# Queries turned in f32, and expert 0's token weights as six rows: a change at the start of an attention and mixture-of-experts kernel

## The chip, the cores and the metric

The kernel runs on one core of one Trainium2 chip. The core has a matrix engine (TensorE, PE in the profile; its weight loads are listed apart as PEld), VectorE (DVE), ScalarE (ACT), GpSimd (POOL) and SyncE (SP). Each works through its own list of instructions in order; semaphores hold one engine until another, or a DMA, is done. DMAs are issued from SP's queue or from POOL's queue here (a single one from ACT's) and are carried by 16 DMA engines. Loads that change the number format on the way (f32 in memory, f16 in the core) are issued from POOL. The metric is device microseconds for one execution; lower is better.

## The reference

The program computes a block-sorted attention and feeds its result to a small mixture of experts:

```python
# attention: B, H, S, D = 4, 8, 768, 64; 8 blocks of 96 rows
P = sort_net                                   # (4, 8, 8, 8)
for _ in range(5):                             # Sinkhorn
    P = exp(P - max(P, -1))
    P = P / sum(P, -1)
    P = P / sum(P, -2)
k_sorted, v_sorted = P @ k_blocks, P @ v_blocks        # mixes whole blocks
attn = softmax(q_blocks @ k_sorted.T / sqrt(D))
x = (attn @ v_sorted)                          # laid out as (3072, 512)
# experts: E, D, F = 4, 512, 1024
p = domain_probs / sum(domain_probs, -1)       # (3072, 4)
out = sum over e of p[:, e] * (relu(x @ w1[e]) @ w2[e])
```

## The kernel before

The order of the instructions is written out by hand; no planner moves them. The work goes through batch elements 0 to 3 one after the other, and inside each through "pairs" or "quads" of heads. Attention of batch element 0 has its own code at the start, in half-blocks, so that the first expert matmuls can begin early; later batch elements' attention is woven between the expert matmuls of the one before. Towards the end only expert matmuls are left.

The change touches only what happens in the first 12 us, before the first attention matmul. There the program does this:

- SP issues, in this order, the load of `sn` (the sorting network, L77), of `p_in` (the domain probabilities with 24 tokens on each partition, L170) and of `p_own` (L171): the probabilities of batch element 0's 768 tokens, placed so that token number t*128+p is on partition p. In `p_own` each piece in memory is the four probabilities of one token, 16 bytes, so this load has 768 pieces.
- POOL issues `load_half_queries(0)` (L172; two loads by L152, one for heads 0 to 3 and one for heads 4 to 7, each 64 partitions with four heads' rows, cast to f16 into `q0`, which lives in the memory of the later tile `Tt[3]`), then `load_natural(0, "k", 0)`, builds the identity `ident`, and issues the loads of `v` for quad 0, `k` and `v` for quad 1, and the four pieces of expert 0's first weight matrix (L183). Then it builds masks (L191 to L200) and, from L330, one half of `sn16`. A load on POOL's queue uses one of eight semaphores in turn, so each waits for the one eight before it.
- TensorE runs `warm(84)` (L307, the matmuls are at L276): matmuls on a constant whose result nobody reads. Inside the fifth Sinkhorn round it transposes the first half of the queries (`h_q(0, 0)` and `h_q(1, 0)`, 24 transposes each at L288, f16) and runs `warm(30)`. ScalarE copies each result into `qT0` (L292).
- VectorE and ScalarE run the five Sinkhorn rounds (L310 to L321): an exponential on ScalarE, then two reductions, two reciprocals and two products on VectorE. Between the rounds VectorE does a step of `spread_weights` (L246, L248, L250: the experts' token weights for all tokens, from `p_in`).
- After the fifth round VectorE and POOL each build a half of `sn16` (L330). `r_half(0)` (L379, matmuls at L342) spreads the first half over 128 partitions into the PSUM tile `ps_R`; VectorE's `build_PI0` (L353) makes the mixing matrices from it; and `mix_half` (L521) multiplies `k` and `v` by them. From there TensorE, VectorE and ScalarE hand the work to and fro until the expert matmuls come in (L704 from 18.6 us on).
- `own_weights` (L261 to L266, called at L1435) turns `p_own` into `p_sb`, expert 0's weight for each token of batch element 0. Its product is first used when VectorE evacuates expert 0's output (L748, 31 us).
- `load_half_queries(1)` (L1405) brings the other half of the queries later.

PSUM tiles come from two rings of two buffers each, `psM` (which holds the warm-up tiles, `ps_R` and some of the mixes) and `psA` (which holds the transposed queries and others). The large tile `room` is free until 36 us, when it takes expert 0's output.

## Time and profile before

| what | value |
|---|---|
| median of three runs | 358.08 us (358.04 to 359.21) |
| the profiled execution's own time | 358.21 us |
| its span, first to last instruction | 356.3 us |
| TensorE matmul busy | 350.4 us (98%) |
| VectorE busy | 277.5 us (78%) |
| ScalarE busy | 170.1 us (48%) |
| POOL busy | 137.6 us (39%) |
| granted TensorE clock | 1.00 |
| TensorE busy in 0 to 5, 5 to 10, 10 to 12 us | 3.94, 5.00, 0.76 us |
| DMA landings: `k` quad 0, `v` quad 0, `k` quad 1, `v` quad 1 | 10.3, 12.2, 14.2, 16.1 us |

The span is what the profiler sees between the first and the last instruction; the execution's time is some 1.9 us longer. A busy share is an average over the whole run, so the table says little about the first 12 us, which is a mere 3% of it. For a stage as short as this one the instructions have to be read one after the other, with the column that says how long an engine was idle before an instruction and what ended that idle time. A matmul row's length is that of a whole group; matmuls overlap, so the spacing between them is shorter than the length of one.

### The profile page before, as it was taken

Reading aid. Unit: us, or ns where it says so; the run is one execution under the profiler, and the core shown is the slowest. Engines: PE = TensorE matmul, PEld = TensorE weight load, DVE = VectorE, ACT = ScalarE, POOL = GpSimd, SP = SyncE. Lnnn points to the kernel's source line nnn. Section 1 sums busy time; section 2 is a strip of 40 time slices with the busy share of each in tenths; the row PEclk is TensorE's granted clock in tenths of the full one; section 3 lists DMA queues with packets and bytes.
Section 4 is the critical chain, followed back from the end, with each engine's and each line's share of the span. In section 5 each row is a group of like instructions: output and inputs, shape, how many; then the busy total and the mean of one; then the engine's idle time right before and its main releaser. Section 6 shows DMA issues by size and latency. Waiting matters only on the chain.

```text
span 356.3 us, 9511 instructions
## 1 busy us (share of the span) xinstructions
PE 350.4 (98%) x3948; PEld 305.5 (86%) x3948; DVE 277.5 (78%) x555; ACT 170.1 (48%) x302; POOL 137.6 (39%) x154
## 2 busy tenths in 40 slices
PE   8899999999999999999999999999999999999996
PEld 8686857888888888988899888888888888888886
DVE  5766787779798687778879988896678886588963
ACT  2653330452425445368847259830288611598301
POOL 8766112466022420000626318840068800188400
PEclk9999999999999999999999999999999999999999
DMA  8999999999999999743995410005200014100021
GB/s 104 203 205 230 212 209 194 207 195 167 195 180 166 195 116 203 138 88 44 180 205 91 107 74 0 2 1 136 78 26 3 2 37 141 62 0 2 0 75 46
DMA packets 74762, 40.26 MB, mean 113 GB/s; under 512 B 41568, under 2 KB 70496, under 8 KB 74720
## 3 DMA queue, kind: packets, MB, share of 16 engines
q0 software_dynamic: 38720, 19.93, 43.2%
q1 hardware_dynamic: 35856, 19.67, 27.2%
q8 instruction: 31, 0.51, 0.6%
q14 instruction: 11, 0.09, 0.1%
q10 hardware_dynamic: 144, 0.07, 0.1%
HBM read 41.88 MB, written 6.34 MB: 135 GB/s over the span
## 4 chain that ended last, share of the span: by engine, by line
PE 95%; DVE 3%; issue 0%; DMA 0%; ACT 0%; DVEq 0%
PE ps_h L815 18%; PE ps_Q L1296 18%; PE ps_p L799 12%; PE ps_X L1153 10%; PE ps_Z L1153 7%; PE ps_Q L1153 7%; PE ps_Z L1296 6%; PE ps_h L704 3%; PE ps_o L741 3%; PE ps_p L860 3%; PE ps_a L479 2%; PE ps_s L444 2%; PE ps_k L425 1%; PE ps_v L391 1%; PE ps_mv L521 1%; PE ps_a L593 0%
## 5 line engine op out<-in xcount | busy, mean ns | idle before, releaser
L815 PE MATMUL ps_h<-xT,w 128*128 128x256 f16 x576 | 67.5, 273 | 0.0
L815 PEld LDWEIGHTS <-w 128*128 128x128 f16 x576 | 55.2, 98 | 7.3
L821 DVE SCALAR_TENSOR_TENSOR Hb<-ps_h,pb 128x1024 f16<-128x1024 f32 x34 | 41.5, 1223 | 17.8 <-PE ps_h L815 17.6
L1153 PEld LDWEIGHTS <-w 128*128 128x128 f16 x480 | 43.6, 98 | 4.7
L1166 POOL TENSOR_TENSOR arena<-tmp,pb 128x512 f16<-128x512 f32 x12 | 15.2, 1276 | 65.7 <-PE ps_Z L1153 49.8
L1296 PEld LDWEIGHTS <-Hb 128*128 128x128 f16 x320 | 31.1, 98 | 3.5
L1165 ACT ACTIVATE tmp<-tmp 128x512 f32<-128x512 f32 x46 | 29.0, 632 | 3.9 <-DVE tmp L1203 3.9
L1296 PEld LDWEIGHTS <-Sb 128*128 128x128 f16 x304 | 28.2, 98 | 3.0
L1153 PEld LDWEIGHTS <-arena 128*128 128x128 f16 x312 | 27.7, 98 | 2.8
L451 ACT ACTIVATE ET<-ps_s 96x768 f16<-96x768 f32 x24 | 18.1, 802 | 25.2 <-PE ps_s L444 25.0
L434 ACT CAST kT<-ps_k 64x384 f16<-64x384 f32 x48 | 22.7, 473 | 13.3 <-PE ps_k L425 12.3
L126 POOL DMA_DIRECT2D arena<-in_q_dram x24 | 19.9, 842 | 20.8 <-DMA q_ring<-arena 17.7
L1153 PE MATMUL ps_X<-ET,arena 128*128 128x256 f16 x168 | 25.2, 272 | 0.0
L1296 PE MATMUL ps_Q<-w,Hb 128*128 128x256 f16 x192 | 24.6, 273 | 0.0
L799 PEld LDWEIGHTS <-Hb 128*128 128x128 f16 x232 | 21.9, 98 | 3.0
L1159 DVE SCALAR_TENSOR_TENSOR Hb<-ps_X,pb 128x512 f16<-128x512 f32 x27 | 18.7, 692 | 7.0 <-PE ps_X L1153 7.0
L1173 ACT COPY ps_X<-ps_Z 128x512 f32<-128x512 f32 x27 | 15.4, 571 | 17.8 <-PE ps_Z L1153 17.8
L1153 PE MATMUL ps_Z<-xT,w 128*128 128x256 f16 (+1 forms) x176 | 22.5, 258 | 0.0
L785 DVE TENSOR_TENSOR Sb<-Hb 128x512 f16<-128x512 f16 x33 | 20.6, 646 | 0.0
L1180 ACT COPY tmp<-ps_X 128x512 f32<-128x512 f32 x26 | 15.2, 586 | 9.2 <-PE ps_X L1153 6.6
L1159 DVE SCALAR_TENSOR_TENSOR Hb<-ps_Z,pb 128x512 f16<-128x512 f32 x27 | 18.4, 683 | 1.3 <-PE ps_Z L1153 1.3
L1203 DVE TENSOR_TENSOR tmp<-ps_Q,tmp 128x512 f32<-128x512 f32 x26 | 17.7, 683 | 0.8 <-PE ps_Q L1153 0.8
(270 smaller groups left out, 744.3 us busy)
## 6 DMA issues: line engine op xcount, KB each, us to landing
w<-in_moe_w_dram POOLq DMA_DIRECT2D x4, 1024.0 KB, 27.2
w<-in_moe_w_dram POOLq DMA_DIRECT2D x6, 512.0 KB, 19.7
arena<-in_k_dram POOLq DMA_DIRECT2D x7, 384.0 KB, 7.6
arena<-in_v_dram POOLq DMA_DIRECT2D x7, 384.0 KB, 8.1
vs<-arena SPq DMA_DIRECT2D x36, 66.0 KB, 5.3
arena<-in_q_dram POOLq DMA_DIRECT2D x24, 96.0 KB, 7.5
out_dram<-ob SPq DMA_DIRECT2D x9, 256.0 KB, 2.0
pb<-p_dram SPq DMA_DIRECT2D x4, 512.0 KB, 5.8
```

Source lines behind the costliest of these rows:

```text
L126: nc.gpsimd.dma_start(t[:, h // 2, :, h % 2, :], q[b, h].rearrange("(t p) d -> p t d", p=P))
L434: nc.scalar.copy(kT[ds(D * hh, D), r], pk[ds(D * r, D), hh].rearrange("p a (i c) -> p a i c", c=CP),)
L451: nc.scalar.activation(ETs[2 * (pr % 2) + hh][:, 0:S].rearrange("c (a x) -> c a x", a=2), pss[hh][0:BLK, :, 0:HS], AF.Exp, bias=0.0, scale ...
L785: tt(sm[0], blk(0, 1), blk(1, 1), ALU.add)
L799: nc.tensor.matmul(ps, lhs(e, f), Ts[e][rhs][:, f, :], start=(first and e == es[0] and f == 0), stop=(done and e == es[-1] and f == KH - 1 ...
L815: nc.tensor.matmul(ps[:, f, :], w1sb[e][:, kc, ds((4 * g + f) * P, P)], xT[:, kc, ds(2 * c * P, 2 * P)], start=(kc == 0), stop=(kc == NKC ...
L821: nc.vector.scalar_tensor_tensor(out=Hb[:, homes.get(e, e), ds(4 * g, 4), :], in0=ps[:], scalar=0.0, op0=ALU.max, in1=weights(e).broadcast ...
L1153: nc.tensor.matmul(dst[:, ds(f * cols, cols)], a[lhs][:, k, ds((f0 + f) * P, P)], t[rhs][:, k, :], start=(first and f == 0 and k == 0), st ...
L1159: nc.vector.scalar_tensor_tensor(out=home(i, j), in0=src.rearrange("p (f x) -> p f x", f=m), scalar=0.0, op0=ALU.max, in1=weight(j).broadc ...
L1165: nc.scalar.activation(src, src, AF.Relu, bias=0.0, scale=1.0)
L1203: tt(t12, Q, u2, ALU.add)
L1296: nc.tensor.matmul(ps, lhs(e, f), Ts[e][rhs][:, f, part], start=(first and e == 0 and f == 0), stop=(e == E - 1 and f == KH - 1), skip_gro ...
```

## The change

Five things change, all ahead of the first attention matmul:

1. The first query half of heads 0 to 3 is no longer loaded by POOL with a cast to f16, but by SP as f32 into the same memory (`q32`), second in SP's list, ahead of the domain probabilities.
2. `p_own` is no longer loaded as 768 pieces of 16 bytes. SP loads six rows of 512 numbers (128 tokens by 4 experts each) into `room`, and four f32 matmuls (one for each expert, six rows by 128 columns against a 6x6 identity) turn them into the old layout, in an unused part of the PSUM tile `ps_R`. VectorE copies the 24 columns into `p_own`. The matmuls and the copy stand just ahead of `r_half(0)`.
3. POOL makes an f32 identity of 64x64 (`ident32`) from `ident`.
4. The 24 f16 transposes of heads 0 to 3 become 24 f32 matmuls against `ident32` (`h_q32`), which run right after the first warm-up instead of inside the fifth Sinkhorn round; ScalarE's copy converts their result to f16.
5. The warm-ups shrink from 84 to 60 and from 30 to 20 matmuls.

```diff
+    q32 = q0[0:64].rearrange("p f h r d -> p (f h r d)").bitcast(F32).rearrange("p (h r d) -> p h r d", h=4, r=R)
+    nc.sync.dma_start(q32.rearrange("p h r d -> p h (r d)"), half_queries(0, 0))
     nc.sync.dma_start(p_in, moe_domain_probs.rearrange("(p t) e -> p t e", t=NT))
-    nc.sync.dma_start(p_own, moe_domain_probs[0:S].rearrange("(t p) e -> p t e", p=P))
-    load_half_queries(0)
+    own_rows = room[0:R, 1, :].rearrange("t (p e) -> t p e", e=E)
+    nc.sync.dma_start(own_rows, moe_domain_probs[0:S].rearrange("(t p) e -> t p e", p=P))
+    nc.gpsimd.dma_start(q0[ds(64, 64), 0].rearrange("p h r d -> p h (r d)"), half_queries(1, 0))
     load_natural(0, "k", 0)
     ident = const.tile([P, P], F16, name="ident")
     make_identity(nc, ident)
+    ident32 = room[0:64, 0, 0:64]
+    nc.gpsimd.tensor_copy(ident32, ident[0:64, 0:64])
...
+    def h_q32():
+        ps = psa([P, 2, 512], F32, "ps_q32")
+        for sg in range(2):
+            for r in range(R):
+                for hh in range(2):
+                    nc.tensor.matmul(
+                        ps[ds(D * hh, D), sg, ds(r * 64, 64)], q32[:, 2 * sg + hh, r, :], ident32, start=True, stop=True
+                    )
+        return ps[:, :, 0:R * 64].rearrange("p s (r x) -> p s r x", r=R)
...
-    warm(84)
+    warm(60)
+    ps_q32 = h_q32()
...
         if it == 4:
-            for qd in range(2):
-                h_q(qd, 0, nc.scalar.copy)
-            warm(30)
+            nc.scalar.copy(qT0[0][:, :, 0], ps_q32)
+            h_q(1, 0, nc.scalar.copy)
+            warm(20)
...
+    own_ps = ps_R[:, 0, ds(256, R * E)].rearrange("p (e t) -> p e t", e=E)
+    for e in range(E):
+        nc.tensor.matmul(own_ps[:, e, :], own_rows[:, :, e], ident32[0:R, 0:R], start=True, stop=True)
+    nc.vector.tensor_copy(p_own.rearrange("p t e -> p e t"), own_ps)
     r_half(0)
```

## The prediction

> **What bounds the kernel now.** I read the page's engine shares first, then the chain that ended last, then the timeline of the first 17 us, because everything that the change touches lies there.

> ```profile
> PE 350.4 (98%) x3948; PEld 305.5 (86%) x3948; DVE 277.5 (78%) x555; ACT 170.1 (48%) x302; POOL 137.6 (39%) x154
> ...
> PE 95%; DVE 3%; issue 0%; DMA 0%; ACT 0%; DVEq 0%
> ```

> TensorE carries the end: the chain is 95% PE and no share of it is a DMA. So a saving counts only if it brings TensorE's real work forward, and a delay in front of that work counts in full. The chain's own list, in order of time (start, length, what), shows what holds the first 12 us:

> ```profile
> 0.75 1.53 DMA sn<-in_sort_net_dram
> ...
> 10.64 0.20 DVE scol L319
> 10.86 0.69 DVE sn L330
> 11.55 0.05 issue
> 11.60 0.26 PE ps_R L342 x4
> 11.86 0.55 PE ps_mk L507 x8
> ...
> 12.45 0.57 PE ps_mk L521 x24
> ```

> From the landing of `sn` to 11.55 us this is the Sinkhorn chain on VectorE and ScalarE; the change leaves all of it in place. `r_half(0)` (L342) is the first TensorE work anybody needs. What TensorE does before is warm-up and the first query transposes, with room behind them (timeline: start, length, engine, line):

> ```profile
> 5.72 0.23 DVE L246 TENSOR_REDUCE T<-T 128x24 f32<-128x96 f32 x1
> ...
> 7.73 0.85 PE L288 MATMUL ps_q<-ident,T 64*64 64x64 f16 x48
> ...
> 8.51 1.85 PE L276 MATMUL ps_w<-Hb 128*128 128x128 f16 x30
> ...
> 9.51 1.46 ACT L292 COPY Sb<-ps_q 128x768 f16<-128x768 f16 x2
> ...
> 10.86 0.68 DVE L330 TENSOR_TENSOR sn<-sn,scol 32x512 f16<-32x512 f32 x1
> ...
> 11.60 0.26 PE L342 MATMUL ps_R<-ident,sn 32*128 32x32 f16 x4 [1.24 <-DVE sn L330]
> ...
> 11.97 0.75 DVE L353 TENSOR_TENSOR Sb<-maskk,ps_R 128x256 f16<-128x256 f16 x2 [0.43 <-PE ps_R L342]
> ...
> 16.15 0.57 PE L521 MATMUL ps_mv<-Sb,arena 128*64 128x64 f16 x24
> ```

> The reader should see the 1.24 us that TensorE idles before L342, waiting for VectorE: that is the cover for everything added to TensorE here. Behind L342 there is no cover: VectorE waits for it, then TensorE for VectorE, and so on until TensorE is dense (it is busy all of the 20 us from 40 to 60).

> **The change part by part.** The sum is made against the profiled run: 358.21 us, that is a span of 356.3 and 1.9 around it; the median of the three runs is 358.08, 0.13 lower.

> *Loads.* The first q half for heads 0 to 3 leaves POOL's queue for SP's, uncast; 768 pieces of 16 bytes become six rows. POOL loses one issue (two took 1.46 us, so 0.73) and gains the copy `ident32` (nearest row: L194's copy, 128x128, 0.29), so `k0` is issued 0.73 us earlier, `v0` and all behind it 0.44. POOL's own later work (its half of L330 ended at 12.46, needed by `r_half(1)` at 13.33) moves earlier too, and nobody waits for it. In the load queue one 384 KB load follows another by 1.9 us (`k0`, `v0`, `k1`, `v1` land at 2.71+7.6=10.3, 4.13+8.1=12.2, 4.88+9.3=14.2 and 5.62+10.5=16.1), so dropping 192 KB brings each about 1.0 us forward. First uses are at 12.45, 12.82, 14.40 and 16.15, none with a wait for DMA: worth 0. If `v1`, which lands only 0.03 us before its use, or `k1` (0.2 before) did hold TensorE, the gain is 0.2 at most, because the work queued ahead of each on TensorE ends no sooner.

> On SP the new load stands ahead of the domain probabilities, whose issue slips by one issue (0.40-0.45), 1.21 to 1.66. They landed 1.8 us after issue, at 3.0; L246 can start as late as 5.87 before the Sinkhorn step behind it (6.11) slips. The 384 KB ahead of them cost between nothing and all of a load of that size: an SP store of 256 KB landed in 2.0 us, so 3.0 for this one. Landing is then between 3.5 and 1.21+3.0+1.8=6.0, a stall of 0 to 0.15. I take 0, since the queue was nearly empty then (30 GB/s between 2.5 and 3.0 us). The six rows are needed only near 10 us.

> *Queries on TensorE.* Removed: 24 of 84 and 10 of 30 warm-up matmuls and 24 f16 transposes. Added: 24 f32 matmuls, 64x64, each loading its own weights. Of the 84 warm-ups 38 start in the first 5 us, and the other 46 take 7.63-5.0=2.63, 57 ns each; 60 of them end at 5.0+22x0.057=6.25. No f32 matmul is in this trace. Lower bound: no dearer than an f16 transpose, 0.85/48=18 ns, 0.43 us for 24. Upper bound: weight load and matmul of one transpose, nothing overlapped, 0.11+0.19=0.30 us, 7.2 us. I take 0.11 each, 2.6 us: the length of one 64x64 weight load, since in the built order these matmuls have no weight load of their own that could run ahead, while nothing says that the streaming behind the load is serial too.

> [...]

> Then 24 transposes (0.43), 20 warm-ups (20x57 ns=1.14) and the four matmuls that turn expert 0's weights. Those: as little as L342's spacing, (0.26-0.17)/3=0.03 each, at most 0.12+0.17=0.29 unoverlapped; I take one 128-column weight load, 0.12, so 0.5 of between 0.1 and 1.2. TensorE is through at 6.25+2.6+0.43+1.14+0.5, with 0.15 for the last matmul's way to PSUM: 11.1, between 8.5 and 16.4. It must be through by 11.55: cover 0.45 us, cost 0. ScalarE copies the first result as f32 (0.81 like L582, 0.73 before) and the second: free by 11.2, next needed at 13.05, so 0.

> *The turn of expert 0's weights.* Here a wait is added. The results lie in `ps_R`, and VectorE's new copy stands behind L330 and ahead of `build_PI0` (L353). In the built order `r_half(0)`'s first matmul now waits on VectorE once more than its weight load does: it writes the same PSUM tile that the copy reads. So the chain becomes L330, copy, L342. The copy is 128x24: a 96x8 reciprocal out of PSUM takes 0.20, a 128x6 reduce 0.16, a 128x24 scalar operation 0.30; I take 0.20, with its 0.03 to start 0.23, between 0.19 and 0.35. Nothing hides it: L507's warm-ups and L353 both start from L342 and shift alike. The 0.43 us that VectorE idles before L353 would have hidden it, but the wait sits ahead of L342.

> Sum: +0.23 on 358.21, 358.44; the median may come 0.13 lower. I say 358.4. With the bounds of all steps: from -0.2+0.19, no change, to 16.4-11.55+0.35+0.15, +5.4.

> **The rivals.** *B, TensorE becomes the bound.* If the f32 matmuls are dearer than 0.11+0.45/24=0.13 us each, `r_half(0)` waits for them and every 10 ns more costs 0.24 us. [...] Slower by 0.5% (1.8 us) begins at 0.20 us each. For it: no row bounds such a matmul closely. Against: 48 weight loads and 48 matmuls of that size ran in 0.85 us, so short loads overlap well.

> [...]

> *C, faster.* The front is fed by DMA after all: `v1` lands 0.03 us before TensorE uses it, and the w1 pieces behind (each issued to be used within a few us of landing) would all come 1.0 us sooner. Place: from 14.4 us on; it decides if L521 and the first layer's L704 start at landings rather than behind other engines. At the most -1.0+0.23: 357.4. Against it: POOL, not TensorE, is the only engine with a wait on a load in the first 24 us.

> *D, the Sinkhorn chain stalls* at L246 because the probabilities land late: 0.15 by my bound, some 358.6; a full 1.8 us would need a landing at 7.5.

> *E, the wait is not seen*, the copy being covered: 358.2.

> **How the numbers follow.** My forecast (through in time, +0.2 to +0.5; own range 358.2 to 358.8) 0.55; B 0.29, of which 0.13 is above 360.0; C 0.08; D 0.03; E 0.05. A change of 0.5%, 1.8 us, is about what a measurement of this kernel tells from none. So the chance within it is 0.83, slower 0.14 (B's dear end and a bad D), faster 0.03 (C would have to be twice its size). The range 357.4 to 360.4 reaches to C at its most and into B as far as 0.21 us a matmul, takes in the spread of the runs (358.04 to 359.21), and leaves about 0.13 out, almost all above.

> **What would show it.** In the changed profile: the 24 f32 matmuls starting near 6.3 and done by 9 us; the 128x24 copy right behind L330's work at 11.55; `r_half(0)` at 11.8 instead of 11.60, released by VectorE; `k1` and `v1` landing about a microsecond sooner with the same waits behind. Wrong would be: `r_half(0)` directly behind the f32 matmuls at 12 or later (B), L246 idle for a DMA (D), or later stages starting earlier than now (C).

## The result, and the profile after

| | before | after |
|---|---|---|
| median of seven runs | 358.13 us (358.03 to 359.21) | 361.60 us (359.36 to 366.77) |
| ratio after / before, 95% interval | | 1.0079 (1.0055 to 1.0102) |
| profiled execution / its span | 358.21 / 356.3 us | 361.32 / 359.2 us |
| granted TensorE clock | 1.00 (the profiled execution) | 0.980 to 0.998 (over the runs) |

The changed kernel is 3.5 us slower by the medians; the ratio, which leaves out the one slow run at 366.77, makes it 2.8 us. The prediction was 358.4 with a range up to 360.4, so it was wrong, and wrong on the side where it had put little chance.

The page of the changed kernel looks almost like the one of before, with one new mark: in the row of the granted clock (tenths of full speed, one digit for each 9 us) the second and third digits are 8.

```profile
PE 352.8 (98%) x3946; PEld 307.9 (86%) x3946; DVE 277.8 (77%) x556; ACT 170.2 (47%) x302; POOL 137.6 (38%) x154
...
PEclk9889999999999999999999999999999999999999
...
PE 95%; DVE 2%; DMA 1%; SPq 0%; issue 0%; ACT 0%
```

In the chain that ended last, DMA now has 1%. The chain's list in order of time (start, length, what) names the transfer:

```profile
2.00 4.85 DMA T<-in_moe_domain_probs_dram
```

The timeline of the first 13 us (start, length, engine, line; in brackets the idle time before it and what ended it), with line numbers of the changed kernel: L251 is L246 of before, L347 is L330, L359 is `r_half`, L342 before.

```profile
1.21 0.74 SPq L171 DMA_DIRECT2D T<-in_q_dram  x1
2.00 0.58 SPq L172 DMA_DIRECT2D T<-in_moe_domain_probs_dram  x1
...
6.79 1.44 PE L305 MATMUL ps_q<-room,T 64*64 64x64 f32 x42 [0.75 <-DMA T<-in_q_dram]
...
6.87 0.25 DVE L251 TENSOR_REDUCE T<-T 128x24 f32<-128x96 f32 x1 [0.99 <-DMA T<-in_moe_domain_probs_dram]
...
8.51 1.29 PE L281 MATMUL ps_w<-Hb 128*128 128x128 f16 x20
9.73 2.03 PE L398 MATMUL ps_R<-room 6*128 6x6 f32 x8
...
12.03 0.68 DVE L347 TENSOR_TENSOR sn<-sn,scol 32x512 f16<-32x512 f32 x1
...
12.64 0.18 DVE L399 COPY T<-ps_R 128x24 f32<-128x24 f32 x1
...
12.88 0.25 PE L359 MATMUL ps_R<-ident,sn 32*128 32x32 f16 x4 [1.12 <-DVE T L399]
```

Read it from the bottom. `r_half(0)` starts at 12.88 instead of 11.60. The copy ahead of it costs little; the work before the copy (L347) is itself 1.17 us late, and 0.93 of that goes back to L251, where VectorE stood 0.99 us for the domain probabilities; the rest is two later VectorE steps that took 0.28 and 0.39 instead of 0.21. SP took 0.74 us to issue the query load, the probabilities were issued at 2.00, and their landing took 4.85 us instead of 1.8.

The second loss follows the first. By windows of 1 us (busy time and instruction counts of PE, PEld, DVE, ACT, POOL; then the granted clock, the DMA share and GB/s), of the changed kernel:

```profile
13.00:14.00 1.00, 0.96 (x31) 0.86 (x30) 0.75 (x2) 0.00 (x0) 1.00 (x2) 1.00 1.30 202
14.00:15.00 1.00, 1.00 (x49) 0.90 (x45) 0.19 (x1) 0.48 (x1) 1.00 (x3) 0.69 1.26 210
15.00:16.00 1.00, 1.00 (x12) 0.70 (x12) 0.37 (x1) 0.91 (x2) 0.94 (x2) 0.50 1.25 206
...
20.00:21.00 1.00, 1.00 (x12) 1.00 (x13) 0.36 (x2) 0.81 (x2) 0.62 (x3) 0.50 1.29 199
21.00:22.00 1.00, 1.00 (x23) 1.00 (x21) 0.38 (x3) 0.48 (x1) 0.92 (x2) 0.90 1.26 208
```

and one of these microseconds in the kernel before:

```profile
15.00:16.00 1.00, 0.89 (x18) 0.69 (x19) 0.94 (x3) 0.85 (x2) 0.21 (x1) 1.00 1.24 202
```

The clock falls to half. By the trace's clock records it was half from 14.38 to 21.20 us. TensorE's last dense work (L281) had ended at 9.8; from there to 12.88 it had only the eight slow passes of the four own matmuls (L398; each f32 matmul shows as two records, called passes here).

The third loss is at the end: SP's wait for the last output store (total, times, longest), first in the changed kernel, then in the kernel before.

```profile
SPq L1594 <- DMA out_dram<-oa: 1.2, 1, 1.2
```

```profile
SPq L1573 <- DMA out_dram<-oa: 0.7, 2, 0.5
```

Matched matmul by matmul from the last one back, the two traces give this ledger of the 3.11 us between the profiled executions:

| place | change, us | running delay |
|---|---|---|
| `r_half(0)` starts (late probabilities, copy) | +1.28 | 1.28 |
| stretch at half clock, 14.4 to 21.2 us | +1.57 | 2.85 |
| pauses of TensorE (one at 31 us) that only the execution of before had | -0.38 | 2.47 |
| from 69 us to the last matmul | 0 | 2.47 |
| closing, from the last store's issue to the end: 2.92 in place of 2.47 | +0.45 | 2.92 |
| around the span | +0.19 | 3.11 |

### The profile page after: what moved, and what is told of

Same layout as the page of the kernel before. It is cut to its first block, busy times and chain, and to the rows that moved or that the text cites. A ratio compares the mean times of both kernels' runs of the same rounds, so it can differ in the third digit from the quotient of the medians.

```text
span 359.2 us, 9513 instructions
## 1 busy us (share of the span) xinstructions
PE 352.8 (98%) x3946; PEld 307.9 (86%) x3946; DVE 277.8 (77%) x556; ACT 170.2 (47%) x302; POOL 137.6 (38%) x154
## 4 chain that ended last, share of the span: by engine, by line
PE 95%; DVE 2%; DMA 1%; SPq 0%; issue 0%; ACT 0%
PE ps_h L836 18%; PE ps_Q L1317 18%; PE ps_p L820 12%; PE ps_X L1174 10%; PE ps_Z L1174 7%; PE ps_Q L1174 7%; PE ps_Z L1317 6%; PE ps_o L762 3%; PE ps_h L725 3%; PE ps_p L881 3%; PE ps_a L500 2%; PE ps_s L465 2%; DMA T<-in_moe_domain_probs_dram 1%; PE ps_k L446 1%; PE ps_v L412 1%; PE ps_mk L542 1%
## 5 line engine op out<-in xcount | busy, mean ns | idle before, releaser
L1317 PEld LDWEIGHTS <-Hb 128*128 128x128 f16 x320 | 31.1, 98 | 3.5
L455 ACT CAST kT<-ps_k 64x384 f16<-64x384 f32 x48 | 22.7, 473 | 13.3 <-PE ps_k L446 12.3
L1194 ACT COPY ps_X<-ps_Z 128x512 f32<-128x512 f32 x27 | 15.4, 571 | 17.8 <-PE ps_Z L1174 17.8
```

What stands on the lines that cost most here:

```text
L455: nc.scalar.copy(kT[ds(D * hh, D), r], pk[ds(D * r, D), hh].rearrange("p a (i c) -> p a i c", c=CP),)
L1317: nc.tensor.matmul(ps, lhs(e, f), Ts[e][rhs][:, f, part], start=(first and e == 0 and f == 0), stop=(e == E - 1 and f == KH - 1), skip_gro ...
```

## The experiments

Theory A came from this ledger: the probabilities behind the query load stall the Sinkhorn chain; the own matmuls, 0.51 us each, would bind if that stall were gone; the thin TensorE stretch ahead of `r_half(0)` costs the clock; one load more on SP lengthens the closing. "Delay" is against the profiled execution of before, matched as above.

**The probabilities first.**

```diff
-    nc.sync.dma_start(q32..., half_queries(0, 0))
     nc.sync.dma_start(p_in, ...)
+    nc.sync.dma_start(q32..., half_queries(0, 0))
```

> The changed kernel with one edit: on SP the domain probabilities are issued ahead of the f32 queries. Theory A (the loss is the stall of the Sinkhorn chain at L251, 0.99 us, and, because of it, a TensorE gap from 9.8 to 12.9 us that halves the clock for 6.8 us, some 1.6 us, and the copy ahead of r_half(0), 0.15): L251 waits for nothing, r_half(0) starts at 11.8 instead of 12.88, the granted clock stays at 1.00 through the first 25 us, and the run takes 358.1+0.2 = 358.3. Rival B (the clock falls because of the f32 matmuls and the shorter warm-ups, stall or no stall): r_half(0) at 11.8 too, but the clock is at 0.5 for some 6.8 us between 13 and 21, and the run takes 359.9. Rival C (the stall moves: the queries land later instead and TensorE is through late): r_half(0) after 12.3.

Measured: 360.75 us (359.77 to 363.43), ratio 1.0066 (1.0041 to 1.0092). Its timeline:

```profile
5.72 0.23 DVE L251 TENSOR_REDUCE T<-T 128x24 f32<-128x96 f32 x1
...
8.14 1.44 PE L305 MATMUL ps_q<-room,T 64*64 64x64 f32 x42 [0.88 <-DMA T<-in_q_dram]
...
11.08 2.03 PE L398 MATMUL ps_R<-room 6*128 6x6 f32 x8
...
13.14 0.20 DVE L399 COPY T<-ps_R 128x24 f32<-128x24 f32 x1 [1.47 <-PE ps_R L398]
13.40 0.25 PE L359 MATMUL ps_R<-ident,sn 32*128 32x32 f16 x4 [0.29 <-DVE T L399]
```

The stall at L251 is gone, and `r_half(0)` is later still. Now the query load is the late one (8.14 in place of 6.79), TensorE goes through its list 1.35 us later, and the copy waits 1.47 us for the own matmuls. In the changed kernel two things are late at once; mending one shows the other. Nor did the clock come back, which theory A had expected: seven of the eight runs had 0.990 to 0.995, although TensorE idled only 0.29 us right before `r_half(0)`, behind the slow passes of L398.

**Expert 0's weights as 768 pieces again** (the changed kernel without own matmuls and copy).

```diff
-    nc.sync.dma_start(own_rows, ...)
+    nc.sync.dma_start(p_own, moe_domain_probs[0:S].rearrange("(t p) e -> p t e", p=P))
...
-    for e in range(E):
-        nc.tensor.matmul(own_ps[:, e, :], own_rows[:, :, e], ident32[0:R, 0:R], start=True, stop=True)
-    nc.vector.tensor_copy(p_own.rearrange("p t e -> p e t"), own_ps)
```

> The changed kernel with the six rows undone: the probabilities of batch element 0 loaded as 768 pieces again, no f32 matmuls for them and no copy ahead of r_half(0); the f32 queries stay ahead of the probabilities on SP. Theory A: L251 stalls as in the changed kernel (0.9 to 1.0 us), r_half(0) at 12.75, TensorE idle from 9.8 to 12.75, clock at 0.5 for some 6.8 us: about 361.2. Rival B (the f32 matmuls of the weights are what spoils the clock): stall as before, clock 1.00, 359.3. Rival D (the six rows are the whole loss): 358.1.

Measured: 361.18 (360.41 to 362.14), ratio 1.0068 (1.0042 to 1.0095).

```profile
7.00 0.25 DVE L250 TENSOR_REDUCE T<-T 128x24 f32<-128x96 f32 x1 [1.22 <-DMA T<-in_moe_domain_probs_dram]
...
12.74 0.26 PE L358 MATMUL ps_R<-ident,sn 32*128 32x32 f16 x4 [2.42 <-DVE sn L346]
```

The stall stays, TensorE idles 2.42 us, and the clock is half from 13.78 to 17.19; all five runs lost clock (0.986 to 0.995). The time is that of the changed kernel: the six rows are not what makes it slow.

**The query load alone** (the kernel before, with a load of that size that nobody reads ahead of the probabilities).

```diff
+    ahead = room[0:64, :, 0:R * D]
+    nc.sync.dma_start(ahead, half_queries(0, 0))
     nc.sync.dma_start(p_in, ...)
```

> The kernel before with one addition: a second, unused f32 load of the same query half into free memory, on SP ahead of the domain probabilities. It changes no TensorE work. Theory A (two losses that this load alone makes): L246 waits about 1 us for the probabilities, r_half(0) starts at 12.6 to 12.8 instead of 11.60, and because the warm-up still ends at 10.36 TensorE idles 2.3 us and loses the clock in some executions but not in all; the closing of the program is 0.43 longer, as in each kernel with one SP transfer more. Profiled at clock 1.00: 358.2+1.1+0.4 = 359.7; with a loss of the clock up to 361. Rival D (the stall needs the shorter POOL queue of the changed kernel): no wait at L246, 358.6.

Measured: 361.08 (359.91 to 362.45), ratio 1.0073 (1.0044 to 1.0102): 2.6 us above the kernel before by the medians, and by the ratio nearly as much as the whole change.

```profile
7.53 0.25 DVE L248 TENSOR_REDUCE T<-T 128x24 f32<-128x96 f32 x1 [1.59 <-DMA T<-in_moe_domain_probs_dram]
...
13.19 0.26 PE L344 MATMUL ps_R<-ident,sn 32*128 32x32 f16 x4 [2.57 <-DVE sn L332]
```

`r_half(0)` is late by 1.59, the whole stall, with POOL's queue as it was before. This execution kept its clock (0.999) and took 359.91; of the other three runs, one with 0.999 took 360.07, and those with 0.991 and 0.986 took 362.09 and 362.45. Stall and clock are two prices.

**Fewer warm-ups** (the kernel before with a longer idle stretch ahead of `r_half(0)`, and nothing else).

```diff
-            warm(30)
+            warm(2)
```

> The kernel before with the second warm-up cut from 30 matmuls to 2, and nothing else. No instruction that anybody waits for moves: the dense work of TensorE ends at 8.8 instead of 10.36, r_half(0) stays at 11.60, TensorE idles 2.8 us. Theory A (the gap in TensorE's work is what halves the clock): clock at 0.5 for 3.4 or 6.8 us somewhere between 12 and 21 in most executions, 358.9 to 360 with a wide spread. Rival B (the clock falls only with the f32 matmuls): clock 1.00, 358.2.

Measured: 359.79 (358.46 to 360.76), ratio 1.0030 (1.0014 to 1.0046). `r_half(0)` by the timeline, and two windows:

```profile
11.83 0.26 PE L342 MATMUL ps_R<-ident,sn 32*128 32x32 f16 x4 [2.61 <-DVE sn L330]
```

```profile
12.00:13.00 1.00, 0.97 (x26) 0.88 (x24) 0.75 (x2) 0.00 (x0) 1.00 (x2) 0.87 1.33 200
13.00:14.00 1.00, 1.00 (x43) 1.00 (x38) 0.00 (x0) 0.46 (x1) 0.91 (x2) 0.50 1.31 203
```

All ten runs lost clock. Four at 0.995 took 358.46 to 359.49, four at 0.990 took 359.65 to 360.34, two at 0.986 took 360.56 and 360.76. A step of 0.005 in the mean clock is about 3.6 us at half speed (0.005 x 357 / 0.5), and from the middle of one group to the next it costs 0.6 to 1.1 us. Leaving dead matmuls out made the kernel 1.1 us slower, by the ratio.

**The gap filled** (the changed kernel with 18 dead matmuls between the own matmuls and `r_half(0)`).

```diff
+    for m in range(18):
+        nc.tensor.matmul(ps_fill[:, m % 4, :], dummy, dummy, start=True, stop=True)
     r_half(0)
```

> The changed kernel with 18 more warm-up matmuls (1.0 us) between the four f32 matmuls of expert 0's weights and r_half(0), in the time that TensorE idles there; the stall stays. Theory A (idle TensorE is what costs the clock): r_half(0) still at 12.9, the clock stays at 1.00, and the run takes 358.1+1.3 = 359.4, with a spread like that of the kernel before. Rival B (the f32 matmuls of 2.0 us before it count as idle whatever follows): clock at 0.5 as before the edit, 361.3 to 361.7.

Measured: 360.79 (360.47 to 362.17), ratio 1.0077 (1.0047 to 1.0106). Three of five runs kept a clock of 1.00 (360.47 to 360.79), two had 0.995 (362.13, 362.17). `r_half(0)` stays at 12.84, and the delay at 19 to 29 us is 1.36 in place of 2.85: in these executions filling gives the clock back. The 359.4 of theory A was missed all the same, since a new pause of TensorE, which nothing in the profile releases, took part of the gain away:

```profile
31.85 0.38 PE L572 MATMUL ps_w<-ident,Sb 128*96 128x128 f16 x4 [0.57 <-issue]
```

**The six rows alone** (the kernel before with the rows, the own matmuls and the copy).

```diff
-    nc.sync.dma_start(p_own, ...)
+    nc.sync.dma_start(own_rows, ...)
...
+    nc.gpsimd.tensor_copy(ident32, ident[0:64, 0:64])
...
+    for e in range(E):
+        nc.tensor.matmul(own_ps[:, e, :], own_rows[:, :, e], ident32[0:R, 0:R], start=True, stop=True)
+    nc.vector.tensor_copy(p_own.rearrange("p t e -> p e t"), own_ps)
```

> The kernel before with only the six rows (load, f32 identity, four f32 matmuls behind warm(30), copy ahead of r_half(0)); queries loaded and turned as before. The four matmuls took 2.03 us in the changed kernel and the warm-up ends at 10.36 here, so TensorE is through at 12.4 and not at 11.55. Theory A: no stall at L246, r_half(0) at 12.4 to 12.6 because of these matmuls, clock 1.00: 358.1+0.9 = 359.0. Rival B (sparse f32 matmuls cost the clock): clock at 0.5 somewhere in 13 to 21, 360.5 or more. Rival E (the matmuls are only slow because the clock or the data was late, and take 0.5 here): 358.3.

Measured: 359.66 (359.10 to 362.88), ratio 1.0044 (1.0019 to 1.0068).

```profile
10.15 2.03 PE L384 MATMUL ps_R<-room 6*128 6x6 f32 x8
...
12.22 0.20 DVE L385 COPY T<-ps_R 128x24 f32<-128x24 f32 x1 [0.53 <-PE ps_R L384]
12.47 0.25 PE L345 MATMUL ps_R<-ident,sn 32*128 32x32 f16 x4 [0.29 <-DVE T L385]
```

With no stall to hide them, the own matmuls and the copy put `r_half(0)` 0.87 late. Six of the ten runs kept their clock; four had 0.991 to 0.995.

**One load more** (the kernel before with an 8 KB load that nobody reads, fourth in SP's list).

```diff
     nc.sync.dma_start(p_own, ...)
+    nc.sync.dma_start(room[0:GH, 0, 0:NB * NB], sort_net.rearrange("b h i j -> (b h) (i j)"))
```

> The kernel before with one more transfer in SP's list, an unused load of 8 KB behind the probabilities. Theory T (SP's transfers take eight semaphores in turn, and the program's end waits for the eight one after the other, so one transfer more puts the last store's semaphore at another place in that list): from the issue of the last store to the end of the span 2.93 us as in the changed kernel instead of 2.50, everything before within 0.1, the run 358.2+0.43 = 358.6. Rival (the longer closing comes with the later or slower start): 2.50, 358.2.

Measured: 358.90 (358.47 to 362.36), ratio 1.0021 (1.0002 to 1.0040). Its last matmul is 0.15 us earlier than that of before, and its closing is 2.89 us with this wait:

```profile
SPq L1574 <- DMA out_dram<-oa: 1.2, 1, 1.2
```

**Halves of 64 columns** (the rows alone, each own matmul cut in two, the copy moved behind the first masked weights).

```diff
-        nc.tensor.matmul(own_ps[:, e, :], own_rows[:, :, e], ident32[0:R, 0:R], start=True, stop=True)
-    nc.vector.tensor_copy(p_own.rearrange("p t e -> p e t"), own_ps)
+        for hh in range(2):
+            nc.tensor.matmul(own_ps[ds(64 * hh, 64), e, :], own_rows[:, ds(64 * hh, 64), e], ident32[0:R, 0:R], ...)
...
     build_PI0(nc.vector, 0, h0, 4, ...)
+    nc.vector.tensor_copy(p_own.rearrange("p t e -> p e t"), own_ps)
```

> The six rows alone again (kernel before otherwise), but each of the four matmuls for the weights cut into two of 64 columns for the two halves of the partitions, and VectorE's copy moved behind build_PI0, so that r_half(0) no longer waits for it. Theory A (the 0.51 us of each such matmul comes of its shape: the f32 matmuls of 64 columns that alternate between the halves were spaced 34 ns a pass): 16 passes in 0.5 to 0.6 us, from 10.3 to 10.9, hidden ahead of 11.55; r_half(0) at 11.6, clock 1.00, 358.2 to 358.4. Rival (a six-row f32 matmul costs 0.24 us a pass whatever its width): 16 passes in 3.9 us, r_half(0) at 14.3, 361.

Measured: 360.79 (359.81 to 362.21), ratio 1.0062 (1.0039 to 1.0085), slower than whole matmuls. The time alone would have convicted the halves. The timeline acquits them:

```profile
9.87 1.12 PE L385 MATMUL ps_R<-room 6*64 6x6 f32 x16
11.85 0.26 PE L345 MATMUL ps_R<-ident,sn 32*128 32x32 f16 x4 [0.86 <-DVE sn L333]
...
19.54 0.39 PE L603 MATMUL ps_a<-Sb,ET 96*128 96x65 f16 x7 [0.72 <-issue]
```

Sixteen passes took 1.12 us, 0.07 each and twice the 0.5 to 0.6 us of theory A, and `r_half(0)` waits only for `sn`, 0.25 late. That is no cost of the halves: it came 0.22 and 0.23 late with one load more and with fewer warm-ups too, where, as here, `sn` was there 0.05 to 0.11 later (ScalarE's first step started at 2.35 to 2.41, not 2.30) and two VectorE products took 0.24 to 0.32 in place of 0.21. The loss came later: two pauses without a releaser at 18.8 and 31.1 us (0.9 and 1.0 us from matmul to matmul), and a wait of 0.78 us for a DMA (`w<-arena`) at 195 us. The next two kernels were made for these pauses.

**The count of TensorE's instructions.** First the kernel before with more dead matmuls and nothing else.

```diff
-            warm(30)
+            warm(46)
```

> The kernel before with 46 warm-up matmuls in place of 30 and nothing else: the same count of TensorE instructions, from r_half(0) on, as with the halved rows. The warm-ups end at about 11.35, ahead of r_half(0) at 11.6, so the front costs nothing. Theory K (pauses follow the count of TensorE's instructions): pauses like those of the halved rows, near 18.5 and 30.8 us, 0.5 to 1 us each; 359.0 to 360.5 us with no change in the front. Theory R (they belong to the rows and their DMAs): none, 358.2 us.

Measured: 360.45 (359.47 to 364.70), ratio 1.0077 (1.0045 to 1.0109), 2.1 us above the kernel before, although its `r_half(0)` starts at 11.57 as before. Then the halved rows with eight warm-ups fewer.

```diff
-            warm(30)
+            warm(22)
```

> The kernel before with the six rows, halved own matmuls and late copy, and 22 warm-ups in place of 30, so that TensorE's instructions up to r_half(0) number 8 matmuls more than in the kernel before, and not 16. With 16 more, r_half(0) was only 0.25 late, yet TensorE stood still for 0.9, 1.0 and 1.0 us at 18.8, 31.1 and 193.6 us, 1.3 to 1.5 us after a 16 KB piece of its code had been called for. Theory K (these pauses are TensorE waiting for the next piece of its code, and their places follow the count of its instructions from the start): pauses of 0.3 us or more, if any, fall some 8 matmuls later in the work than in that run, at the same count from the start, and none falls where no piece of code was called for within the 2.4 us before its end. Theory R (they belong to the rows): again at the same places in the work. Front: r_half(0) at 11.6 (own matmuls end at 11.3), so 358.4 us without pauses, up to 360.5 with three.

Measured: 359.11 (358.14 to 361.95), ratio 1.0031 (1.0009 to 1.0053). A pause of each, first with 46 warm-ups, then the halved rows with 22:

```profile
30.67 0.33 PE L548 MATMUL ps_w<-ident,Sb 128*96 128x128 f16 x3 [0.72 <-issue]
```

```profile
14.60 0.31 PE L531 MATMUL ps_mv<-Sb,arena 128*64 128x64 f16 x7 [1.09 <-issue]
```

Counted from the start of the program, the pauses of these runs come after 223 matmuls (halved rows with 22), 351 and 607 (halved rows), 607 (46 warm-ups), 606 (filled gap) and, for 0.3 us each, 351 and 607 in the kernel before itself. These are 128 and 256 apart, and the 607th matmul is 16 further on in the work of the kernel before than in the others. So the place goes by the count (theory K of the expectation), not by the rows. Both kernels missed part of it: a second pause, at 351, was expected with 46 warm-ups and did not come, and with 22 the one pause came at 223, a place that had not been named. The execution with 22 also lost one step of clock (half from 17.26 to 20.67 us), some 0.9 us. The other loss with 46 warm-ups is a wait of 1.36 us for `w<-arena` at 194.9 us, where the kernel before waited for nothing. Why these late transfers come later in some kernels is open.

**The query part, well ordered** (the changed kernel, probabilities first, expert 0's weights as 768 pieces).

```diff
-    nc.sync.dma_start(q32..., half_queries(0, 0))
     nc.sync.dma_start(p_in, ...)
+    nc.sync.dma_start(q32..., half_queries(0, 0))
-    nc.sync.dma_start(own_rows, ...)
+    nc.sync.dma_start(p_own, ...)
...
```

> The changed kernel with the probabilities issued ahead of the float32 query load, and expert 0's weights again as 768 small pieces (no own matmuls, no copy): the query part alone, in the other order on SP. Theory A (the loss is the late probabilities, the own matmuls and what the clock makes of them; the query part itself is harmless where it is ordered behind): no stall at L250, the query load lands about 8.1, the 24 float32 matmuls and the warm-ups end by 11.2, r_half(0) starts at 11.6 to 11.8, the clock stays 1.00, the closing is 0.43 longer; 358.6 us. Rival C (the query load is late enough that TensorE becomes the bound): r_half(0) at 12.5 or later, 359.5 us or more.

Measured: 358.52 (358.42 to 360.21), ratio 1.0004 (0.9991 to 1.0018); nine of ten runs had a clock of 0.998 to 1.00.

```profile
7.66 1.44 PE L304 MATMUL ps_q<-room,T 64*64 64x64 f32 x42 [1.79 <-DMA T<-in_q_dram]
...
11.74 0.26 PE L358 MATMUL ps_R<-ident,sn 32*128 32x32 f16 x4 [1.07 <-DVE sn L346]
```

Turning the queries in f32 did no harm in this kernel, where its load stands behind the probabilities and no own matmuls follow it on TensorE (358.52 against 358.35 for the kernel before). It brought nothing either.

**All three mends** (the changed kernel with the probabilities first, halved own matmuls and the late copy, by the edits above).

> The changed kernel with three mends: the probabilities ahead of the query load, the own matmuls cut into halves of 64 columns (1.12 us in place of 2.03 in an earlier run), the copy behind the first masked weights. Theory A: TensorE is through with the queries at 9.6 and the 20 warm-ups at 11.1, the halves end at 12.2, r_half(0) starts at 12.2 to 12.4 without the copy's 0.2 us; 0.7 from the front, 0.43 from the closing, clock 1.00: 359.4 us, 1.3 below the changed kernel with the first mend alone (360.75). Rival (the clock falls whatever fills the gap, or the halves are dear behind the float32 transposes): r_half(0) at 13 or later or a clock of 0.995, 360.3 us or more.

Measured: 359.36 (358.72 to 361.24), ratio 1.0028 (1.0012 to 1.0043).

```profile
11.85 0.26 PE L359 MATMUL ps_R<-ident,sn 32*128 32x32 f16 x4 [0.40 <-DVE sn L347]
```

`r_half(0)` came earlier than the 12.2 to 12.4 expected, as the query load landed at 7.25 and not at 8.0. The delay is 0.28 at 25 us and -0.10 at 95 us; after that its profiled execution, the slowest of its ten, waited 0.70, 0.65 and 0.62 us for transfers at 116, 125 and 180 us. Six of the ten runs, with clocks of 0.999 or 1.00, lie between 358.7 and 359.5. Against the kernel before in the same runs (358.35) 1.0 us of the change's 3.5 is left. No version found here beats the kernel before.

## Why the prediction was wrong

*Loads: the step that failed.* It took "0" for the stall at L246, out of "a stall of 0 to 0.15". The stall was 0.99 us (1.00, 1.22 and 1.59 in the three other kernels with this order), and with two slower VectorE steps behind it (0.24) and the copy (0.11) `r_half(0)` came 1.28 late. The mechanism stood there as rival D, and its slope held ("a full 1.8 us would need a landing at 7.5"; the step started at 6.87, one microsecond behind the 5.87 up to which there was room). But the landing was bounded by 6.0, and D got 0.03 of the chance. Two terms were mis-sized. The issue in front took 0.74 us, not "0.40-0.45": one price was used for all SP loads. And the two landings were bounded from loads that had the engines nearly to themselves, "since the queue was nearly empty then". That was the window which the new load itself would fill; behind it POOL's `q` and `k` loads came into the same 16 engines (274 GB/s from 4 to 6 us, where the kernel before had 181 and 165), and the query load needed 5.5 us, not at most 3.0. A row of the kernel before bounds it better: POOL's load of the same query half, issued at 1.28, landed only 4.08 us later. The order runs show the cause: no stall with the probabilities first, the full stall with a load that nobody reads in front of them. That it is the sharing with POOL's loads which makes 5.5 out of 3.0 was read from the transfer records and not tried.

The other side of this step was right. `k` and `v` landed at 8.5, 10.5, 13.4 and 15.4 us in place of 10.3, 12.2, 14.2 and 16.1, 0.8 to 1.8 us sooner, and this was worth nothing; nor did it bring anything in the well ordered query part, where they landed 0.5 to 1.6 us sooner and `r_half(0)` started at 11.74. Rival C falls.

*Queries on TensorE.* The 24 f32 matmuls were priced too high: 0.11 each against 1.6 us together, 0.068 each. They show as two records each (x48 in all, 34 ns apart). The reason given for 0.11, that they have no weight load which could run ahead, did not hold: the trace lists 48 weight loads for them, 0.135 us each, and all start within 1.4 us, so they overlap. The dear end of B, 0.20 us a matmul and more, is shown by no run. The 0.15 for the last matmul's way to PSUM was an estimate without a row; the 30 warm-ups of the kernel before give 0.14 (1.85 us in all, 30x57 ns=1.71 by their spacing). The own matmuls were priced too low: 0.12, "at most" 0.29, against 0.51. Both bounds came from f16 rows and did not hold for f32 with 128 columns. In the changed kernel that was free, since TensorE was through at 11.76 and `sn` came at 12.71. Without the stall it decides: `r_half(0)` at 13.40 with the probabilities first, 12.47 with the rows alone. So rival B was real, in the four own matmuls and not in the 24, and rival D hid it.

*The turn of expert 0's weights.* The added wait was where it was predicted, and smaller: L347 ends at 12.71 and `r_half(0)` starts 0.17 later, where 0.06 passed before; +0.11 and not +0.23. Rival E falls.

*What the sum lacked.* Two terms. First the clock, +1.57: the prediction cut ten warm-ups, counted TensorE's idle time as cover, and never asked what idle time does to TensorE's clock. The one run of seven that kept 0.998 took 359.36; the ledger without the clock gives 358.21+1.28-0.38+0.45 = 359.56, or 359.75 with the 0.19 around the span. That is inside the range, but for another reason than the one given. Second the closing, +0.45, for one load more on SP: the eight kernels with it close in 2.89 to 2.93 us, the five with as many as before in 2.47 to 2.50 (the one with two warm-ups is left aside: the issue of its last store took 0.77 us in place of 0.33, and it closed in 3.14).

What stays open is the share of each term in any one run: clock and late waits differ from run to run, so the ledger is that of one execution.

## What to carry to other kernels

Keep a small load that heads a serial chain ahead of a big one on its queue (behind one, the chain here stalled for 0.99 to 1.59 us), and bound its landing with every queue running, not with the traffic that the trace shows in the window which the new load will fill. Idle time ahead of the bound engine is cover for new work, but on TensorE it was here also a risk to the clock: with 2.61 us of it all ten runs lost some, in steps of 3.41 us at half clock. Where two kernels differ by 1 or 2 us, find the place in the traces before blaming the edit: sixteen dead matmuls that did not delay `r_half(0)` cost 2.1 us by the medians.

## What the runs showed of the hardware

**TensorE seems to wait for its own code.** The page of the profile lists a queue named for instructions; this is the line of the changed kernel (packets, MB, share):

```profile
q8 instruction: 31, 0.51, 0.6%
```

That is 16 KB a piece (0.51 MB in 31). With 46 warm-ups the transfers of the first pieces began at 9.96, 16.01, 21.94 and 28.45 us, one every 6 us, while TensorE begins 90 to 150 matmuls, each with a weight load, in that time. Where TensorE paused, it went on 2.2 to 2.4 us after such a start (28.45 to 30.67; 12.20 to 14.60 in the halved rows with 22; 17.24 to 19.59 and 29.20 to 31.43 for the two short pauses of the kernel before). That these pieces are its code and what it waited for is read from these places and times; no view names it. What decides whether a piece comes early enough is open. In the profiled execution of the changed kernel no such pause was seen, so it has no part in the ledger's loss.

**The price of the f32 matmuls here differed with the form of their weights.** A pass with weights of 6x128 took 0.25 us (2.03 for 8 in the changed kernel), of 6x64 0.07 (1.12 for 16 in the halved rows), of 64x64 0.034 (the 48 of the changed kernel). The 6-row forms read every fourth number of a row, the 64x64 one reads them in a row; whether it is that or the width was not separated beyond the halves.

**The closing was longer with one SP transfer more.** SP's transfers use eight semaphores in turn, and in the records of the program's end SP passes these eight one after the other, 0.06 us apart where none is waited for. With one load more (the changed kernel), the last store's is the first of them: it lands at 357.84, and the other seven are passed from 357.92 to 358.29. In the kernel before, the last store's was the last of them, and the others were passed by 354.83, ahead of its landing at 355.35. More than one load more was not tried.
